# Moving the second batch's first pair forward: loads, transposes and scores in a fused attention and MoE kernel

## The chip, the cores and the metric

The kernel runs on one core of one Trainium2 chip. The metric is the device time of one execution in microseconds. Before the change the median of 7 runs is 318.27 us (317.29 to 319.65). One execution was also taken by the hardware profiler; all durations below come from it.

## What is computed

Attention with a few global tokens, followed by a two-layer feed-forward with a hard-swish gate. There are 8 batches of 8 heads, 512 local and 32 global positions, head size 64. Cut to what matters:

```python
s_g = scale * q_g @ concat(k_g, k_l).T          # global queries see all keys
out_g = softmax(s_g) @ concat(v_g, v_l)
s_ll = where(|i - j| <= 32, scale * q_l @ k_l.T, -1e9)   # local window
s_l = concat(scale * q_l @ k_g.T, s_ll)
out_l = softmax(s_l) @ concat(v_g, v_l)
x = concat(out_g, out_l) per token               # [8 * 544, 512]
h = x @ w_in                                     # 512 -> 2048
out = (h * clip(h + 3, 0, 6) / 6) @ w_out        # 2048 -> 512
```

## The kernel before, in words

Work is cut into 32 pairs p of two heads: p = 4 b + m, with b the batch and m the pair of heads in it. Pairs 0 to 3 are the first batch, pairs 4 to 7 the second. An order written out by hand covers the first two batches and is what the change edits; from pair 8 on a loop does the rest.

The steps of a pair are functions. `load` (L117) issues the DMAs of k, q and v on SP's queue into one of 16 staging buffers; `cast` (L131) turns them into 16-bit tiles kn, qn and vt; `vshift` (L142) makes a copy of v shifted by half a block, vb. `emit_T` (L216) transposes kn and qn on TensorE and copies them from PSUM: k by VectorE into kT (L229), q by ScalarE into qT (L232), with a small wrapped copy (L237 for the second batch). `emit_S(p, ch)` (L299) makes the scores of one of two chunks: two mask matmuls (L281), eight score matmuls (L293), two exps on ScalarE (L297). `emit_AV` (L324) multiplies with v and divides by the sums on VectorE (reciprocal L344, product L345, giving xn). `emit_X` (L387) transposes xn on TensorE (L398) and copies it to xt on VectorE (L402). For the global tokens `load_g`, `cast_G` (L191) and `emit_G` (L201, L209) bring keys and queries in; `kglob` (L211) copies the global keys of a batch into its kT, and `vglob` (L146) the global values into its vb. `emit_SG` (L303) makes the scores of the global queries, `emit_TD` (L241) transposes a later pair by DMA.

The feed-forward of a batch is cut into units. `u1(c)` (L421) is one of 16 columns of the first layer: four matmuls over m (L426), one activation t on ScalarE (L431), one product gt on VectorE (L433). It can be split over m: the first HEAD columns are started with m = 0, 1 and completed as the first batch's xt come in ("heads"). `u2(t, c4)` (L438) is a quarter of an output tile: four matmuls (L442). `M(n)` takes the next n units from a list. First-layer weights are 16 tiles; `load_w` and `cast_w` (L163, L174) bring them in, and columns 4 to 7 need tiles 4 to 7, and so on by fours. Output weights are 16 more tiles, cast on POOL.

Each engine runs its instructions in the order in which the code emits them. SP issues all loads in one order; POOL does nearly all casts in another; TensorE, ScalarE and VectorE follow the written order of steps. PSUM is seven buffers of one bank each for all steps: a step takes a free one and waits for the engine that empties it. Before the change ScalarE casts weight tiles 4 to 7, all eight first weight tiles are loaded ahead of pair 4, and pair 4's transposes follow u1(6).

Of the kernel before, what the change touches and what calls it, by code (L numbers as in the profile page):

```python
# [14 lines left out]
def kernel(  # L15
# [12 lines left out]
    nc = tc.nc  # L28
# [13 lines left out]
    qk_scale = 1.0 / math.sqrt(D)  # L42
# [3 lines left out]
    EXP = mybir.ActivationFunctionType.Exp  # L46
# [65 lines left out]
    st = {}  # L112
# [4 lines left out]
    def load(p, what="kqv"):  # L117
        b, m = divmod(p, NM)
        s = st.setdefault(p, {})
        for c in what:  # L120
            src = {"k": k_l, "q": q_l, "v": v_l}[c]
            t = stage()
            if c != "v" and b < NRUN:
                nc.sync.dma_start(out=t.rearrange("p (h x) -> p h x", h=2),  # L124
                                  in_=src[b, 2 * m:2 * m + 2].rearrange("h (p j) d -> p h (j d)", j=NT))
            else:
                nc.sync.dma_start(out=t.rearrange("p (h kb d) -> p (h kb) d", h=2, kb=NT),
                                  in_=src[b, 2 * m:2 * m + 2].rearrange("h (kb p) d -> p (h kb) d", p=P))
            s[c + "f"] = t.rearrange("p (h kb d) -> p kb h d", h=2, kb=NT)

    def cast(p, what, eng):  # L131
        b, m = divmod(p, NM)
        s = st[p]
        for c in what:
            if c == "v":
                o = vts[b % NV][:, :, m, vc].rearrange("p kb (h d) -> p kb h d", h=2)
            else:
                s[c + "n"] = wrk.tile([P, NT, P], FP16, tag=c + "n", name=c + "n", bufs=4)
                o = s[c + "n"].rearrange("p kb (h d) -> p kb h d", h=2)
            eng.tensor_copy(out=o, in_=s[c + "f"])  # L140
# [27 lines left out]
    def cast_w(kind, i, eng):  # L168
        if kind == "in":
            qd, m = divmod(i, NM)  # L170
            o = w_in_t[m][:, qd * 512:(qd + 1) * 512]
        else:
            o = w_out_t[i // 4][:, i % 4]
        (eng.copy if eng is nc.scalar else eng.tensor_copy)(out=o, in_=w_st[kind, i])  # L174
# [5 lines left out]
    def load_g(b0, b1, nm):  # L180
        src = {"kg": k_g, "qg": q_g}[nm]
        t = stage()
        nc.sync.dma_start(
            out=t[:, 0:(b1 - b0) * HH * D].rearrange("p (n d) -> p n d", d=D),
            in_=src[b0:b1].rearrange("b (x y) s d -> (y s) (b x) d", x=HH))
        gst[b0, nm] = t

    def cast_G(b0, b1, nm, eng=nc.vector):
        n = wrk.tile([P, 4 * P], FP16, tag="gn", name=nm + "n", bufs=2)
        nb = b1 - b0  # L190
        eng.tensor_copy(out=n[:, 0:nb * P], in_=gst[b0, nm][:, 0:nb * P])  # L191
        gst[b0, nm, "n"] = n
# [18 lines left out]
    def kglob(b, eng):  # L211
        kv = kTs[b % 2][:, :, 0:NT * KW].rearrange("p m (u c) -> p m u c", u=NT)
        eng.tensor_copy(out=kv[:, :, :, P:KW],
                        in_=kgT[:, :, b].unsqueeze(2).to_broadcast([P, NM, NT, Sg]))

    def emit_T(p, qdve=False):  # L216
        b, m = divmod(p, NM)
        s = st[p]
        kT = kTs[b % 2][:, m]
        kv = kT[:, 0:NT * KW].rearrange("p (u c) -> p u c", u=NT)  # L220
        qT = wrk.tile([P, Sl + W], FP16, tag="qT", name="qT", bufs=5)
        ps = {}
        for c in "kq":
            ps[c] = ps_tile("psT" + c, FP16)[:, 0:Sl]
            for j in range(NT):
                nc.tensor.matmul(out=ps[c][:, j * P:(j + 1) * P], lhsT=s[c + "n"][:, j], rhs=ident,
                                 is_transpose=True)
        qcopy = nc.vector.tensor_copy if qdve else nc.scalar.copy
        nc.vector.tensor_copy(  # L229
            out=kv[:, :, 0:P].rearrange("p u (i j) -> p u i j", j=NT),  # L230
            in_=ps["k"].rearrange("p (j u i) -> p u i j", j=NT, u=NT))
        qcopy(out=qT[:, W:Sl + W].rearrange("p (i j) -> p i j", j=NT),  # L232
              in_=ps["q"].rearrange("p (j i) -> p i j", j=NT))
        if b == 0:
            nc.vector.tensor_copy(out=qT[:, 0:W], in_=qT[:, Sl:Sl + W])
        else:
            nc.scalar.copy(out=qT[:, 0:W].rearrange("p (i j) -> p i j", j=NT),  # L237
                           in_=ps["q"].rearrange("p (j i) -> p i j", j=NT)[:, P - W // NT:P])
        s["qT"], s["kT"] = qT, kT
# [41 lines left out]
            nc.tensor.matmul(out=pss[e], lhsT=ident, rhs=mneg[:, ch], start=True, stop=False,  # L281
                             skip_group_check=True)

    def emit_Ss(p, ch):
        s = st[p]
        qT, kT, pss = s["qT"], s["kT"], s["ps", ch]
        if "E" not in s:
            s["E"] = wrk.tile([P, 2, 2, Sl], FP16, tag="E", name="E", bufs=3)
        for w in range(NT):
            c0 = w * KW if ch == 0 else ((w - 1) % NT) * KW + D  # L290
            for e in range(2):
                r = slice(e * D, (e + 1) * D)
                nc.tensor.matmul(out=pss[e][:, w * P:(w + 1) * P], lhsT=kT[r, c0:c0 + P],  # L293
                                 rhs=qT[r, w * P:(w + 1) * P], start=False, stop=True,
                                 skip_group_check=True)
        for e in range(2):
            nc.scalar.activation(out=s["E"][:, ch, e], in_=pss[e], func=EXP, scale=qk_scale)  # L297

    def emit_S(p, ch):  # L299
        emit_Sm(p, ch)  # L300
        emit_Ss(p, ch)
# [85 lines left out]
    def emit_X(p):  # L387
        b, m = divmod(p, NM)
        xn = st[p]["xn"]
        if b > 3 or (b == 3 and m < NM - 1):  # L390
            xt = wrk.tile([P, Sl], FP16, tag=f"xt{m}", name=f"xt{m}", bufs=2)
            xts.setdefault(b, []).append(xt)
            nc.sync.dma_start_transpose(out=xt.rearrange("p (w c) -> p w c", w=NT),
                                        in_=xn.rearrange("p w c -> p (w c)"))
            return
        psX = ps_tile("psX", FP16)
        for w in range(NT):
            nc.tensor.matmul(out=psX[:, w * P:(w + 1) * P], lhsT=xn[:, w], rhs=ident,  # L398
                             is_transpose=True)
        xt = wrk.tile([P, Sl], FP16, tag=f"xt{m}", name=f"xt{m}", bufs=2)  # L400
        xts.setdefault(b, []).append(xt)
        nc.vector.tensor_copy(out=xt, in_=psX[:, 0:Sl])  # L402
# [68 lines left out]
    def M(n):  # L471
        for _ in range(n):
            if units:
                units.pop(0)()
# [16 lines left out]
    load(3, "kq")  # L491
    for p in range(1, NM):
        load(p, "v")
    for i in range(8):
        load_w("in", i)
    load(4, "kq")
    load_g(1, 4, "kg")
    load(5, "kq")
    for i in range(8, 12):
        load_w("in", i)  # L500
    load(6, "kq")
    load(4, "v")
    load(5, "v")
    load(7, "kq")
    for i in range(12, NC):
# [41 lines left out]
    def ones_v(i, eng):  # L547
        for c in (1, 2 + P):
            eng.memset(vbs[i][0:P - W, :, :, c:c + 1], 1.0)
            eng.memset(vts[i][:, :, :, c:c + 1], 1.0)  # L550
# [16 lines left out]
    def first(p, what="kqv"):  # L567
        cast(p, what, nc.gpsimd)
        vshift(p, nc.gpsimd)
# [6 lines left out]
        first(p, "v")  # L576
    for i in range(4):
        cast_w("in", i, nc.gpsimd)
    ones_v(1, nc.gpsimd)
    vglob(1, nc.gpsimd)  # L580
    cast(4, "kq", nc.gpsimd)
    cast(5, "kq", nc.gpsimd)
    for i in range(8, 12):
        cast_w("in", i, nc.gpsimd)
    cast(6, "kq", nc.gpsimd)
    first(4, "v")
    first(5, "v")
    cast(7, "kq", nc.gpsimd)
    for i in range(12, NC):
# [13 lines left out]
    u1 = units.pop(0)  # L603
# [19 lines left out]
    emit_S(3, 0)  # L623
    emit_AV(1)
    emit_S(3, 1)
    for i in range(4, 8):
        cast_w("in", i, nc.scalar)
    emit_X(1)
    emit_AV(2)
    HEAD = 4  # L630
    for c in range(HEAD):
        u1(c, range(2))
    emit_X(2)
# [1 line left out]
    for c in range(HEAD):  # L635
        u1(c, range(2, 3))
    emit_X(3)
    for c in range(HEAD):
        u1(c, range(3, 4))
    u1(4)  # L640
    u1(5)
    u1(6)
    emit_T(4)
    cast_G(1, 4, "kg")
    emit_T(5)
    emit_G(1, 4, "kg")
    emit_S(4, 0)
    u1(7)
    kglob(1, nc.vector)
    u1(8)  # L650
    emit_S(4, 1)
    emit_T(6)
    u1(9)
    emit_S(5, 0)
    emit_AV(4)
    u1(10)
    emit_S(5, 1)
    emit_X(4)
    u1(11)
    emit_T(7)  # L660
    emit_S(6, 0)
    emit_AV(5)
    u1(12)
    emit_S(6, 1)
    emit_S(7, 0)
    emit_X(5)
    emit_AV(6)
    for t in Egs:
        nc.vector.memset(t[:, NT], 0.0)
    cast_G(0, 4, "qg")  # L670
    u1(13)
    emit_S(7, 1)
    emit_X(6)
    emit_G(0, 4, "qg")
    u1(14)
    emit_AV(7)
    u1(15)
    emit_SG(0)
    emit_SG(1)
    M(1)  # L680
    emit_TD(2 * NM)
    load(2 * NM + 1)
    cast(2 * NM + 1, "kq", nc.gpsimd)
# [1 line left out]
    emit_X(7)  # L685
    sum_E(0)
    sum_E(1)
    M(1)
    emit_SG(2)
    emit_SG(3)  # L690
    vglob(2, nc.gpsimd)
    kglob(2, nc.gpsimd)
    held = [units.pop(0), units.pop(0)]
    u2 = moe_units(lambda mm: xts[1][mm], Sl, local_dests(1))
    units[:0] = u2[0:NC]
# [144 lines left out]
```

## Time and profile before

| | |
|---|---|
| median of 7 runs | 318.27 us |
| profiled execution | 318.91 us |
| its span, first to last instruction | 317.1 us |
| TensorE busy, VectorE, ScalarE, POOL | 305.2, 212.7, 201.6, 152.0 us |
| granted TensorE clock | 1.00 |
| loads in the first 70 us | 18.25 MB at a mean of 261 GB/s |

Times in the rows are microseconds from the start of the span. A row of the timeline has the start, the time taken, the engine, the line, the operation, the tiles written and read, the shapes, and how many instructions were merged; square brackets hold the idle time of the engine before it and what ended that. A DMA row in the chain of waits runs from its issue to its landing. PE is TensorE, PEld its weight loads, DVE VectorE, ACT ScalarE, POOL GpSimd, SP the engine that issues loads.

### The profile page before, as it was taken

How to read it: one execution, taken by the hardware profiler on the slowest of the kernel's cores; microseconds unless marked ns; L12 is line 12 of the kernel's file. 1: busy time of each engine (PE TensorE's matmuls, PEld its weight loads, DVE VectorE, ACT ScalarE, POOL GpSimd, SP SyncE). 2: the span in 40 equal slices, each digit the busy share in tenths (PEclk: the TensorE clock that was granted, in tenths of full speed). 3: DMA queues.
4: the chain of work that ended last, by engine and by line, in shares of the span. 5: the costliest groups of instructions: out<-in, count | busy, mean ns of one | idle time of the engine just before them, and what ended most of it. 6: DMA issues, size and time to landing. Idle time of an engine off the chain costs nothing.

```text
span 317.1 us, 7319 instructions
## 1 busy us (share of the span) xinstructions
PE 305.2 (96%) x2673; PEld 162.0 (51%) x2673; DVE 212.7 (67%) x485; ACT 201.6 (64%) x420; POOL 152.0 (48%) x270
## 2 busy tenths in 40 slices
PE   7996999999999899999999999999999999999995
PEld 5553455545555454555555555555555554448444
DVE  6758678898665998568956896458834962389101
ACT  6757886886444895479844994589656941579000
POOL 4776788469976685575585456543410000000000
PEclk9999999999999999999999999999999999999999
DMA  7999999999999997999999997897542002100131
GB/s 211 266 283 315 253 290 276 250 173 224 179 241 204 207 226 152 189 207 189 198 174 210 209 185 155 203 198 123 112 114 86 17 19 83 66 2 1 35 99 66
DMA packets 140260, 53.05 MB, mean 167 GB/s; under 512 B 127552, under 2 KB 131904, under 8 KB 140224
## 3 DMA queue, kind: packets, MB, share of 16 engines
q1 hardware_dynamic: 138048, 52.32, 76.0%
q0 software_dynamic: 2176, 0.26, 1.3%
q8 instruction: 21, 0.34, 0.5%
q14 instruction: 15, 0.12, 0.2%
HBM read 35.13 MB, written 8.91 MB: 139 GB/s over the span
## 4 chain that ended last, share of the span: by engine, by line
PE 60%; DMA 14%; POOL 11%; DVE 5%; issue 3%; SPq 3%; ACT 2%; POOLq 0%; ACTq 0%
PE po L442 28%; PE psH L426 25%; DMA stg<-in_v_l_dram 8%; DMA stg<-in_moe_w_out_dram 4%; DVE gt L433 3%; POOL vt L140 2%; PE psS L268 2%; DMA stg<-in_k_l_dram 2%; POOL vb L144 2%; SPq L124 2%; PE pav L340 1%; PE pav L337 1%; DVE E L275 1%; POOL vb L147 1%; PE po L454 1%
## 5 line engine op out<-in xcount | busy, mean ns | idle before, releaser
L442 PE MATMUL po<-wout,gt 128*128 128x512 f16 x528 | 122.8, 379 | 0.0
L426 PE MATMUL psH<-xt,win 128*128 128x512 f16 x512 | 119.2, 379 | 2.8 <-DVE gt L433 2.1
L433 DVE SCALAR_TENSOR_TENSOR gt<-t,psH 128x512 f16<-128x512 f32 (+1 forms) x144 | 89.8, 652 | 23.0 <-ACT t L431 21.9
L431 ACT ACTIVATE t<-psH,half_col 128x512 f32<-128x512 f32 (+1 forms) x144 | 91.6, 669 | 14.7 <-PE psH L426 12.9
L426 PEld LDWEIGHTS <-win 128*128 128x128 f16 x576 | 53.1, 98 | 54.7 <-issue 2.8
L442 PEld LDWEIGHTS <-gt 128*128 128x128 f16 x528 | 48.4, 98 | 51.9
L275 DVE TENSOR_TENSOR E<-E,mk 128x512 f16<-128x512 f16 x96 | 50.3, 557 | 30.4 <-ACT E L272 28.8
L272 ACT ACTIVATE E<-psS 128x512 f16<-128x512 f32 x96 | 49.8, 604 | 13.7 <-PE psS L268 13.6
L446 ACT COPY ot<-po 128x512 f32<-128x512 f32 x16 | 9.4, 585 | 58.7 <-PE po L442 53.1
L140 POOL CAST kn<-stg 128x512 f16<-128x512 f32 x31 | 20.1, 647 | 31.8 <-DMA stg<-in_k_l_dram 31.3
L363 POOL TENSOR_TENSOR s<-Eg 128x128 f32<-128x128 f16 x24 | 10.7, 446 | 36.9 <-ACT Eg L312 35.9
L446 DVE COPY ot<-po 128x512 f32<-128x512 f32 x17 | 11.7, 690 | 23.1 <-PE po L442 23.0
L345 DVE TENSOR_TENSOR xn<-pav,rc 128x256 f16<-128x256 f32 x64 | 26.0, 421 | 1.3
L140 POOL CAST qn<-stg 128x512 f16<-128x512 f32 x31 | 19.7, 636 | 11.7 <-DMA stg<-in_q_l_dram 11.4
L140 POOL CAST vt<-stg 128x512 f16<-128x512 f32 x32 | 20.5, 641 | 8.0 <-DMA stg<-in_v_l_dram 7.3
L144 POOL COPY vb<-vt 64x512 f16<-64x512 f16 x32 | 20.0, 625 | 2.1
L297 ACT ACTIVATE E<-psS 128x512 f16<-128x512 f32 x32 | 17.1, 609 | 4.9 <-PE psS L293 4.7
L337 PE MATMUL pav<-vt,E 128*128 128x65 f16 x256 | 20.0, 194 | 0.0
L340 PE MATMUL pav<-vb,E 128*128 128x65 f16 x256 | 20.0, 195 | 0.0
L337 PEld LDWEIGHTS <-E 128*128 128x128 f16 x256 | 17.8, 99 | 3.4
L340 PEld LDWEIGHTS <-E 128*128 128x128 f16 x256 | 16.9, 97 | 2.9
L268 PEld LDWEIGHTS <-kT 64*128 64x128 f16 x384 | 10.8, 94 | 9.9 <-issue 9.2
(93 smaller groups left out, 277.3 us busy)
## 6 DMA issues: line engine op xcount, KB each, us to landing
stg<-in_k_l_dram SPq DMA_DIRECT2D x32, 256.0 KB, 3.6
stg<-in_q_l_dram SPq DMA_DIRECT2D x32, 256.0 KB, 4.2
stg<-in_v_l_dram SPq DMA_DIRECT2D x32, 256.0 KB, 4.7
out_dram<-ot SPq DMA_DIRECT2D x23, 256.0 KB, 3.9
stg<-in_moe_w_in_dram SPq DMA_DIRECT2D x16, 256.0 KB, 5.7
stg<-in_moe_w_out_dram SPq DMA_DIRECT2D x16, 256.0 KB, 4.9
out_dram<-ot SPq DMA_DIRECT2D x8, 192.0 KB, 4.0
out_dram<-ot SPq DMA_DIRECT2D x16, 64.0 KB, 1.9
```

Of the source, the lines that this page charges most:

```text
L140: eng.tensor_copy(out=o, in_=s[c + "f"])
L144: eng.tensor_copy(out=vbs[b % NV][0:D, :, m, vc], in_=vts[b % NV][D:P, :, m, vc])
L272: nc.scalar.activation(out=E[:, ch, e], in_=pss[2 * ch + e], func=EXP, scale=qk_scale)
L275: nc.vector.tensor_tensor(out=E[:, ch, e], in0=E[:, ch, e], in1=mk[:, ch].rearrange("p w c -> p (w c)"), op=mult)
L337: nc.tensor.matmul(out=o, lhsT=E[:, 0, e, w * P:(w + 1) * P], rhs=vt[:, w, m, c], start=True, stop=False, skip_group_check=True)
L340: nc.tensor.matmul(out=o, lhsT=E[:, 1, e, w * P:(w + 1) * P], rhs=vb[:, (w - 1) % NT, m, c], start=False, stop=True, skip_group_check=True)
L345: nc.vector.tensor_tensor(out=xn[:, 2 * w2:2 * w2 + 2].rearrange("p w (e d) -> p w e d", e=2), in0=po[:, :, 1:1 + P].rearrange("p w (e d) ...
L426: nc.tensor.matmul(out=ps[:, 0:n], lhsT=w_in_t[m][:, c * P:(c + 1) * P], rhs=rhs(m), start=(m == 0), stop=(m == NM - 1), skip_group_check= ...
L431: nc.scalar.activation(out=t1[:, 0:n], in_=ps[:, 0:n], func=RELU, bias=half_col, scale=1.0 / 6.0)
L433: nc.vector.scalar_tensor_tensor(out=gts[c][:, 0:n], in0=t1[:, 0:n], scalar=1.0, in1=ps[:, 0:n], op0=amin, op1=mult)
L442: nc.tensor.matmul(out=po[t][:, 0:dm], lhsT=gts[c][:, t * P:(t + 1) * P], rhs=w_out_t[c // 4][:, c % 4], start=(c == 0), stop=(c == NC - 1))
L446: (nc.scalar.copy if t % 2 else nc.vector.tensor_copy)(out=ot, in_=po[t][:, 0:dm])
```

## The change

In SP's order, pair 4's k and q and the global keys of batches 1 to 3 go ahead of weight tiles 4 to 7, and pair 4's v goes ahead of tiles 8 to 11. POOL's order follows: it casts pair 4's k and q after tile 3, then tiles 4 to 7 (before on ScalarE), pair 5's k and q, pair 4's v, and only then the constant columns and global values of the second batch's vb. On TensorE three columns are started as heads instead of four; pair 4's transposes stand between the first batch's last X and the heads' last matmuls; the global keys follow u1(3). A new step `emit_S4` makes the scores of both chunks of a pair in one run: four mask matmuls, sixteen score matmuls, four exps. The columns u1 are spread differently between the steps of pairs 4 to 7, and the first two output units move behind X(7) and SG(3).

```diff
--- before.py
+++ after.py
@@ -281,7 +281,7 @@
             nc.tensor.matmul(out=pss[e], lhsT=ident, rhs=mneg[:, ch], start=True, stop=False,
                              skip_group_check=True)
 
-    def emit_Ss(p, ch):
+    def emit_Ss(p, ch, exps=True):
         s = st[p]
         qT, kT, pss = s["qT"], s["kT"], s["ps", ch]
         if "E" not in s:
@@ -293,8 +293,21 @@
                 nc.tensor.matmul(out=pss[e][:, w * P:(w + 1) * P], lhsT=kT[r, c0:c0 + P],
                                  rhs=qT[r, w * P:(w + 1) * P], start=False, stop=True,
                                  skip_group_check=True)
+        if exps:
+            emit_Se(p, ch)
+
+    def emit_Se(p, ch):
+        s = st[p]
         for e in range(2):
-            nc.scalar.activation(out=s["E"][:, ch, e], in_=pss[e], func=EXP, scale=qk_scale)
+            nc.scalar.activation(out=s["E"][:, ch, e], in_=s["ps", ch][e], func=EXP, scale=qk_scale)
+
+    def emit_S4(p):
+        emit_Sm(p, 0)
+        emit_Sm(p, 1)
+        emit_Ss(p, 0, False)
+        emit_Ss(p, 1, False)
+        for ch in range(2):
+            emit_Se(p, ch)
 
     def emit_S(p, ch):
         emit_Sm(p, ch)
@@ -491,15 +504,17 @@
     load(3, "kq")
     for p in range(1, NM):
         load(p, "v")
-    for i in range(8):
+    for i in range(4):
         load_w("in", i)
     load(4, "kq")
     load_g(1, 4, "kg")
+    for i in range(4, 8):
+        load_w("in", i)
     load(5, "kq")
+    load(4, "v")
     for i in range(8, 12):
         load_w("in", i)
     load(6, "kq")
-    load(4, "v")
     load(5, "v")
     load(7, "kq")
     for i in range(12, NC):
@@ -576,14 +591,16 @@
         first(p, "v")
     for i in range(4):
         cast_w("in", i, nc.gpsimd)
+    cast(4, "kq", nc.gpsimd)
+    for i in range(4, 8):
+        cast_w("in", i, nc.gpsimd)
+    cast(5, "kq", nc.gpsimd)
+    first(4, "v")
     ones_v(1, nc.gpsimd)
     vglob(1, nc.gpsimd)
-    cast(4, "kq", nc.gpsimd)
-    cast(5, "kq", nc.gpsimd)
     for i in range(8, 12):
         cast_w("in", i, nc.gpsimd)
     cast(6, "kq", nc.gpsimd)
-    first(4, "v")
     first(5, "v")
     cast(7, "kq", nc.gpsimd)
     for i in range(12, NC):
@@ -623,11 +640,9 @@
     emit_S(3, 0)
     emit_AV(1)
     emit_S(3, 1)
-    for i in range(4, 8):
-        cast_w("in", i, nc.scalar)
     emit_X(1)
     emit_AV(2)
-    HEAD = 4
+    HEAD = 3
     for c in range(HEAD):
         u1(c, range(2))
     emit_X(2)
@@ -635,49 +650,44 @@
     for c in range(HEAD):
         u1(c, range(2, 3))
     emit_X(3)
+    emit_T(4)
     for c in range(HEAD):
         u1(c, range(3, 4))
+    cast_G(1, 4, "kg")
+    u1(3)
+    emit_G(1, 4, "kg")
+    kglob(1, nc.vector)
     u1(4)
+    emit_S4(4)
+    emit_T(5)
     u1(5)
+    emit_S4(5)
     u1(6)
-    emit_T(4)
-    cast_G(1, 4, "kg")
-    emit_T(5)
-    emit_G(1, 4, "kg")
-    emit_S(4, 0)
+    emit_AV(4)
+    emit_T(6)
     u1(7)
-    kglob(1, nc.vector)
+    emit_X(4)
+    emit_S4(6)
     u1(8)
-    emit_S(4, 1)
-    emit_T(6)
+    emit_AV(5)
+    emit_T(7)
     u1(9)
-    emit_S(5, 0)
-    emit_AV(4)
+    emit_X(5)
+    emit_S4(7)
     u1(10)
-    emit_S(5, 1)
-    emit_X(4)
-    u1(11)
-    emit_T(7)
-    emit_S(6, 0)
-    emit_AV(5)
-    u1(12)
-    emit_S(6, 1)
-    emit_S(7, 0)
-    emit_X(5)
     emit_AV(6)
     for t in Egs:
         nc.vector.memset(t[:, NT], 0.0)
     cast_G(0, 4, "qg")
-    u1(13)
-    emit_S(7, 1)
+    u1(11)
     emit_X(6)
     emit_G(0, 4, "qg")
-    u1(14)
+    u1(12)
     emit_AV(7)
-    u1(15)
+    u1(13)
     emit_SG(0)
     emit_SG(1)
-    M(1)
+    u1(14)
     emit_TD(2 * NM)
     load(2 * NM + 1)
     cast(2 * NM + 1, "kq", nc.gpsimd)
@@ -685,11 +695,13 @@
     emit_X(7)
     sum_E(0)
     sum_E(1)
+    u1(15)
     M(1)
     emit_SG(2)
     emit_SG(3)
     vglob(2, nc.gpsimd)
     kglob(2, nc.gpsimd)
+    M(1)
     held = [units.pop(0), units.pop(0)]
     u2 = moe_units(lambda mm: xts[1][mm], Sl, local_dests(1))
     units[:0] = u2[0:NC]
```

## The prediction

> **What bounds the kernel now.** I read the page first, then the windows of ten microseconds, the timeline of each engine up to 60 us, and last the chain that ended last. TensorE is busy for 305.2 of 317.1 us, and its idle time sits in few places:
>
> ```profile
> PE 305.2 (96%) x2673; PEld 162.0 (51%) x2673; DVE 212.7 (67%) x485; ACT 201.6 (64%) x420; POOL 152.0 (48%) x270
> ...
> 20.00:30.00 10.00, 7.11 (x61) 3.73 (x59) 7.02 (x16) 7.66 (x15) 7.07 (x13) 1.00 1.00 314
> 30.00:40.00 10.00, 9.16 (x91) 4.66 (x92) 6.80 (x16) 7.26 (x14) 6.91 (x12) 1.00 1.03 262
> 40.00:50.00 10.00, 10.00 (x136) 5.94 (x135) 7.82 (x27) 7.83 (x16) 9.12 (x16) 1.00 1.05 296
> ```
>
> The columns are the stretch, then PE, PEld, DVE, ACT, POOL busy, the granted clock, the DMA share and GB/s. TensorE lacks 2.9 + 0.8 = 3.7 us between 20 and 40 us, the place that the change works on. There the DMA engines are full and the clock is 1.00. The timelines of TensorE and ScalarE show why it idles:
>
> ```profile
> 22.91 1.32 ACT L174 CAST win<-stg 128x512 f16<-128x512 f32 x2 [0.82 <-DMA stg<-in_moe_w_in_dram]
> 24.14 4.15 ACT L431 ACTIVATE t<-psH,half_col 128x512 f32<-128x512 f32 x7
> 30.05 0.34 PE L201 MATMUL psGT<-ident,kgn 128*128 128x128 f16 x3 [1.71 <-DVE kgn L191]
> 34.21 0.40 PE L293 MATMUL psS<-qT,kT 64*128 64x128 f16 x8 [0.79 <-DVE kT L213]
> ```
>
> ScalarE casts weights until 24.1, so its seven t (L431), the seven gt of VectorE behind them and the cast kgn behind those come late, and the transposes of the global keys wait 1.71 us. From 34.2 to 106.7 us TensorE has no gap the profile lists, but one weight tile arrives with nothing to spare. In the chain of waits:
>
> ```profile
> 54.42 5.32 DMA stg<-in_moe_w_out_dram
> ...
> 59.79 0.62 POOL wout L174
> ...
> 60.46 0.38 PE po L442
> ```
>
> The last output weight lands at 59.74 and is cast by 60.4; its matmul starts at 60.46, though its unit began at 59.61 and would have reached it at 60.25. Since the DMA engines are full and the same loads precede this weight before and after, whatever TensorE gains ahead of this point ends here. The most it can win is nothing; it can lose.
>
> **The loads and POOL.** All loads go through SP's one queue in order, so a transfer that is moved takes another's place in the stream. The weight tile after the fourth lands at 20.80 (its cast on ScalarE starts at 20.83); pair 4's k takes that place, lands near 20.9 instead of 24.3, and its q near 21.6 instead of 25.1. Weight tiles 4 to 7 move to the places up to 25.7. Pair 4's v takes the place of the first of tiles 8 to 11 and lands near 28.1. POOL takes over four casts from ScalarE (0.62 us each there, 0.61 here). Its row that matters:
>
> ```profile
> 21.18 1.88 POOL L147 COPY vb<-vg 32x2048 f16<-32x2048 f16 x1
> ```
>
> Before, this copy (vglob) and the column memsets fill POOL's wait for pair 4's k. After, they stand behind pair 4's v. From 28.1 POOL has no wait left: v and its shift 1.35, memsets 0.43, vglob 1.93, four casts at 0.64 = 2.56, pair 6's k and q 1.25. The sum is 7.5, so pair 6's q is ready at 35.6, where it was at 33.1. The eighth weight tile is cast at 26.3 instead of 24.2.
>
> **TensorE up to pair 6.** Prices from rows: u1 0.86; a pair's transposes 0.46; the mask matmuls 0.95 for four at once; one chunk's scores 0.33; AV 0.50; X 0.23. Three heads end their first two parts at 19.5 and X(2), AV(3), X(3) end at 21.8. T(4) waits for its q, done at 22.6; the last head parts end at 23.2, u1(3) at 24.1. VectorE's kgn stands behind kT and three gt, and ScalarE's t behind the qT copies (0.54): gt from 24.0 at 0.6 each, kgn done near 26.2. So the 1.71 us wait stays, at about 2.1. Then come G, u1(4) to 27.2, the four scores runs of pair 4 to 28.8, T(5) 29.3, u1(5) 30.2, pair 5's scores about 31.9 (its qT stands behind four exps on ScalarE), u1(6) 32.7, AV(4) 33.2. T(6) needs POOL's q at 35.6: a wait of some 2.2 us, and T(6) ends at 35.9. Before it ended at 35.0, with more done. What is left from there to a common mark (first batch-1 work complete: all sixteen u1, X(7), SG(0) and SG(1), no output unit) is nine u1 7.8, four X 0.9, two score sets 3.2, three AV 1.5, T(7) 0.5, the global queries 0.2 and SG 0.3, together 14.4: the mark would be reached at 50.3. Before, the second output unit starts at 51.13 with one unit of 0.86 ahead of it, so its mark is 50.27. Up to here the change is worth nothing.
>
> **What the single run of scores costs.** emit_S4 queues four exps on ScalarE before the next u1's t, and gt of that u1 stands before the reciprocals of the AV that follows, in VectorE's queue. The rows:
>
> ```profile
> 9.03 2.07 ACT L297 ACTIVATE E<-psS 128x512 f16<-128x512 f32 x4
> 10.95 0.63 ACT L232 COPY qT<-psTq 128x512 f16<-128x512 f16 x1
> ...
> 36.91 0.69 DVE L433 SCALAR_TENSOR_TENSOR gt<-t,psH 128x512 f16<-128x512 f32 x1 [1.25 <-ACT t L431]
> 37.51 0.18 DVE L344 RECIPROCAL rc<-pav 128x4 f32<-128x4 f32 x1
> 37.72 0.42 DVE L345 TENSOR_TENSOR xn<-pav,rc 128x256 f16<-128x256 f32 x1
> 38.06 0.17 DVE L344 RECIPROCAL rc<-pav 128x4 f32<-128x4 f32 x1
> 38.27 0.42 DVE L345 TENSOR_TENSOR xn<-pav,rc 128x256 f16<-128x256 f32 x1
> ```
>
> Four exps hold ScalarE for 1.92 us; t takes 0.69; from the start of gt to the end of xn are 1.78 us. From the start of the first chunk's scores: 0.43 until the exps start, 1.92, 0.69, 0.04, 1.78, so xn is there after 4.86 and X is through at 5.0. Pair 6's scores are followed on TensorE by the second chunk 0.33, u1(8), AV(5), T(7), u1(9) and X(5), which would be through at 3.57: a wait of 1.4 us. Before, AV(5) follows an S of two exps with gt already done, and the profile lists no wait. Pair 7's scores are followed by u1(10), AV(6), u1(11) and X(6), through at 3.11: a wait of 1.9 us. The cast of the global queries follows xn on VectorE (memsets 0.13, cast 0.39), so their transposes wait 0.3 more, and X(7), behind gt, xt, four copies of 1.2, gt and xn, 0.15. Together 3.8 us: the mark falls at 54.0.
>
> **Sum.** 54.04 - 50.27 = 3.77 us, less the 0.2 us wait for the last weight tile, which a later TensorE no longer has: +3.6 us. TensorE has no listed gap from there to 106.7 us, so nothing takes it back; the wait of 1.52 us at 108.3 ends on gt, behind ScalarE and TensorE themselves, and moves along. The span becomes 320.7 us and the profiled run 318.91 + 3.6 = 322.5; against the median of 318.27, 321.8 us. Casts taken off ScalarE (4 x 0.62) are no gain, as they delayed only work that now waits for kgn or POOL.
>
> **Bounds.** Not shown before is which PSUM buffers the run of four takes. Best, buffers long free: nothing. Worst, pair 6's and 7's last mask waits for a buffer that gt or xt holds (free 0.9 and 1.0 us after the masks could end): +1.9. I take nothing, since three or four of seven are free by my times. DMA landings jump by up to 1.2 us in the stream (30.80 after 29.12, where 0.65 to 0.8 is usual), so POOL's 35.6 is worth 0.8 either way. Downstream, POOL's copy of 1.88 us at 104.3 lies beside VectorE's mask products (2.94 us for three, 0.51 for one before); a shifted TensorE may miss it and lose up to the 1.5 + 0.4 us of waits at 108.3 and 120.1: down to +3.6 - 0.8 - 1.9 = +0.9; up to +3.6 + 0.8 + 1.9 = +6.3 if all worst come together.
>
> The clock is 1.00 in all windows, through the gap of 1.71 us, so I charge no clock for gaps of 2.2. The Trainium skill (TensorE: Matmul & The Clock Gate, "What's actually happening") says that an idle window of about 3.4 us halves TensorE's clock until a busy one has passed. By that rule a POOL later by 1.2 us would cost an estimated 1.7 us more, and my sum would be +5.3; no gap in this trace is long enough to show it.
>
> **Rivals.** *The waits for xn do not come* (the four exps run far enough ahead, or DVE's rows are shorter): the mark is 50.3 and the last weight tile pins the rest; 318.3 us. Against it: t, gt and xn are queued in the order of the code on both engines in the trace. Chance 0.12. *Faster*: the phase shift removes the waits of 1.52 and 0.41 us at 108.3 and 120.1, since POOL's 1.88 us copy no longer stands beside the mask products. Price 1.9 us, in VectorE's stage at 103 to 108 us; it decides only if the front part loses under 1 us. 318.3 - 1.9 = 316.4 us. For it: DVE took 0.98 us per product there and 0.50 elsewhere. Against it: a loss of 3.6 ahead. Chance 0.07. *More loss* by PSUM buffers held: 318.27 + 5.5 = 323.8 us; for it, two T, four S and one u1 are seven of seven buffers. It is in the slower case. *The loads do not come earlier*: T(4) then waits to 25.8 ahead of the heads, 3.2 us more before kgn; POOL's wait for pair 6 covers about 2.2, so some 1 us is added.
>
> **How the numbers follow.** Slower by over 0.3% (0.95 us, about what a measurement of this kernel can tell from no change): 0.81, all cases with the waits for xn. Within: 0.12. Faster: 0.07. The range reaches from no change, 318.2, to 323.8, the loss with held buffers; faster at 0.07 and the far ends stay out.
>
> **What would show it.** Right: ScalarE rows of four exps (L297) at pairs 4 to 7; TensorE waits at psX (L398) on xn of 1 to 2 us, twice, near 42 and 48 us; a wait of T(6) on POOL's kn or qn near 35; kgn again a wait near 26; the last output weight landing near 59.7 with no stall on it; the later waits unchanged. Wrong: no psX waits, output weights that land earlier than 59, or a first output unit near 50.

## The result, and the profile after

The changed kernel takes 323.51 us (median of 12 runs, 321.44 to 326.51) beside 318.98 us of the kernel before (31 runs): ratio 1.0138, 95% interval 1.0114 to 1.0163, that is 3.6 to 5.2 us slower. The forecast was +3.6 us and 321.8 us. The profiled execution after has a span of 320.9 us, with 322.65 us for the run. The totals hardly move:

```profile
PE 305.8 (95%) x2673; PEld 162.7 (51%) x2673; DVE 212.7 (66%) x485; ACT 198.8 (62%) x416; POOL 153.9 (48%) x274
...
20.00:30.00 10.00, 7.92 (x82) 4.46 (x81) 7.33 (x20) 4.29 (x9) 6.46 (x12) 1.00 1.08 342
30.00:40.00 10.00, 8.17 (x91) 4.48 (x89) 4.67 (x10) 7.62 (x17) 9.74 (x19) 1.00 1.08 295
40.00:50.00 10.00, 6.73 (x81) 3.52 (x78) 5.59 (x18) 5.92 (x12) 9.58 (x18) 1.00 1.00 275
```

The first line is from the page, the others are the windows of ten microseconds. Four casts went from ScalarE to POOL. TensorE gains 0.8 us between 20 and 30 us and loses 1.0 and 3.3 us in the next two windows, where POOL is nearly full. The timeline of TensorE names the waits (in brackets: idle time before, and what ended it):

```profile
26.97 0.34 PE L201 MATMUL psGT<-ident,kgn 128*128 128x128 f16 x3 [1.80 <-DVE kgn L191]
35.62 0.40 PE L226 MATMUL psTk<-ident,kn 128*128 128x128 f16 x4 [1.46 <-POOL kn L140]
42.86 0.28 PE L411 MATMUL psX<-ident,xn 128*128 128x128 f16 x2 [1.01 <-DVE xn L358]
43.40 0.28 PE L411 MATMUL psX<-ident,xn 128*128 128x128 f16 x2 [0.26 <-DVE xn L358]
48.88 0.29 PE L411 MATMUL psX<-ident,xn 128*128 128x128 f16 x2 [1.45 <-DVE xn L358]
49.43 0.28 PE L411 MATMUL psX<-ident,xn 128*128 128x128 f16 x2 [0.26 <-DVE Eg L680]
50.18 0.40 PE L201 MATMUL psGT<-ident,qgn 128*128 128x128 f16 x4 [0.47 <-DVE qgn L191]
```

Line numbers are up to 13 higher after the change: L302 is the exps, L411 the transposes of X, L444 is t, L446 gt, L358 xn. The two pairs of psX rows are new; the wait on kgn is still there, a little longer. How xn comes late is read down the ScalarE and VectorE timelines:

```profile
38.89 2.06 ACT L302 ACTIVATE E<-psS 128x512 f16<-128x512 f32 x4 [0.73 <-PE psS L293]
40.81 0.71 ACT L444 ACTIVATE t<-psH,half_col 128x512 f32<-128x512 f32 x1
...
41.56 0.69 DVE L446 SCALAR_TENSOR_TENSOR gt<-t,psH 128x512 f16<-128x512 f32 x1 [2.34 <-ACT t L444]
42.16 0.17 DVE L357 RECIPROCAL rc<-pav 128x4 f32<-128x4 f32 x1
42.37 0.42 DVE L358 TENSOR_TENSOR xn<-pav,rc 128x256 f16<-128x256 f32 x1
```

Four exps take ScalarE from 38.89 to 40.81; t waits behind them; VectorE idles 2.34 us for t with gt at the head of its queue, and the reciprocals of AV(5), whose matmuls ended near 40.5, start at 42.16. X(5) needs xn and waits.

### The profile page after: what moved, and what is told of

Read it like the earlier page. It is cut to its first block, busy times and chain, and to the rows that moved or that the text cites. A ratio compares the mean times of both kernels' runs of the same rounds, so it can differ in the third digit from the quotient of the medians.

```text
span 320.9 us, 7313 instructions
## 1 busy us (share of the span) xinstructions
PE 305.8 (95%) x2673; PEld 162.7 (51%) x2673; DVE 212.7 (66%) x485; ACT 198.8 (62%) x416; POOL 153.9 (48%) x274
## 4 chain that ended last, share of the span: by engine, by line
PE 76%; DVE 7%; DMA 5%; ACT 4%; POOL 2%; issue 2%; SPq 1%; POOLq 0%
PE po L455 35%; PE psH L439 29%; DMA stg<-in_q_l_dram 4%; PE psS L268 3%; DVE gt L446 3%; DMA stg<-in_k_l_dram 2%; PE pav L350 2%; PE pav L353 2%; DVE xn L358 1%; ACT t L444 1%; DVE E L275 1%; PE psSG L324 1%; ACT E L302 1%; PE po L467 1%; PE pg L390 1%
## 5 line engine op out<-in xcount | busy, mean ns | idle before, releaser
L446 DVE SCALAR_TENSOR_TENSOR gt<-t,psH 128x512 f16<-128x512 f32 (+1 forms) x144 | 90.0, 650 | 27.4 <-ACT t L444 26.2
L444 ACT ACTIVATE t<-psH,half_col 128x512 f32<-128x512 f32 (+1 forms) x144 | 91.7, 670 | 19.0 <-PE psH L439 17.9
L140 POOL CAST kn<-stg 128x512 f16<-128x512 f32 x31 | 19.0, 614 | 32.3 <-DMA stg<-in_k_l_dram 29.1
L376 POOL TENSOR_TENSOR s<-Eg 128x128 f32<-128x128 f16 x24 | 10.8, 452 | 35.7 <-ACT Eg L325 34.9
L140 POOL CAST vt<-stg 128x512 f16<-128x512 f32 x32 | 21.7, 679 | 11.3 <-DMA stg<-in_v_l_dram 10.9
L358 DVE TENSOR_TENSOR xn<-pav,rc 128x256 f16<-128x256 f32 x64 | 26.0, 421 | 1.3
L144 POOL COPY vb<-vt 64x512 f16<-64x512 f16 x32 | 20.7, 648 | 2.1
L302 ACT ACTIVATE E<-psS 128x512 f16<-128x512 f32 x32 | 17.0, 603 | 5.8 <-PE psS L293 5.7
```

What stands on the lines that cost most here:

```text
L144: eng.tensor_copy(out=vbs[b % NV][0:D, :, m, vc], in_=vts[b % NV][D:P, :, m, vc])
L358: nc.vector.tensor_tensor(out=xn[:, 2 * w2:2 * w2 + 2].rearrange("p w (e d) -> p w e d", e=2), in0=po[:, :, 1:1 + P].rearrange("p w (e d) ...
L444: nc.scalar.activation(out=t1[:, 0:n], in_=ps[:, 0:n], func=RELU, bias=half_col, scale=1.0 / 6.0)
L446: nc.vector.scalar_tensor_tensor(out=gts[c][:, 0:n], in0=t1[:, 0:n], scalar=1.0, in1=ps[:, 0:n], op0=amin, op1=mult)
```

## The experiments

Theory A is the prediction's: gt, queued behind four exps on one side and ahead of AV's reciprocals on the other, makes xn and so X late. Rival B is that POOL and the loads set the pace and the wait on xn is only where it shows.

Two measures serve throughout: the ratio to the kernel before, timed on the same chip, and in the profile the mark of the prediction (all sixteen u1, X(7), SG(0) and SG(1) done). In the changed order the first output unit starts at the mark. Before it was 50.27, after it is 55.03.

**The changed kernel again.**

> The changed kernel once more, beside the other runs of this call. Both theories: ratio to the kernel before 1.011 to 1.016. Its profile tells whether the first 18 us of the profiled run after, in which TensorE was 1.0 us later than before ahead of every edit, belong to the change: if not, the scores of pair 3 start near 16.1 us again and the mark (X(7), u1(15), SG(0), SG(1) done) falls near 54.0; if so, 17.1 and 55.0 again.

Ratio 1.0133 (1.0099 to 1.0167). X(0) starts at 14.28 us, near the 14.03 of before and not at the 14.98 of the profile after, so that early delay is of single executions. The mark was at 56.69 and the span 322.6 us all the same, and the windows show a reason that neither profile of the first comparison has:

```profile
36.00:38.00 2.00, 1.84 (x13) 0.93 (x14) 1.23 (x4) 0.67 (x2) 1.87 (x4) 0.82 0.99 290
38.00:40.00 2.00, 2.00 (x9) 0.80 (x7) 1.02 (x2) 0.69 (x1) 2.00 (x5) 0.50 1.02 237
40.00:42.00 2.00, 2.00 (x27) 1.24 (x27) 0.00 (x0) 1.17 (x3) 1.94 (x5) 0.83 0.93 206
```

After a wait of 2.08 us on pair 6's k the granted clock (third number from the end) falls; 0.82, 0.50 and 0.83 make a stretch at 0.50 from 37.3 to 40.7 us. Half of 3.4 us is 1.7 us of TensorE's time. The two spans differ by as much (322.6 and 320.9), though X(0) was 0.7 us earlier here and the wait on pair 6's k 0.6 us longer.

**u1 ahead of the scores.**

```diff
-    emit_S4(6)
-    u1(8)
+    u1(8)
+    emit_S4(6)
...
-    emit_S4(7)
-    u1(10)
+    u1(10)
+    emit_S4(7)
```

> u1(8) ahead of pair 6's scores and u1(10) ahead of pair 7's, so that their t and gt no longer stand behind four exps and ahead of the reciprocals of AV(5) and AV(6). Theory A (order of the queues): the psX waits on xn (1.0 + 0.3 and 1.45 + 0.3 us) shrink to under 0.5 us together, and the kernel is 2.3 to 3.3 us faster than the changed one, ratio to before 1.003 to 1.007. Rival B (TensorE waits there for work that POOL and the loads bring late, and the xn wait is only where it shows): the wait moves to other rows, the gain stays under 1 us, ratio at or over 1.010.

Ratio 0.9996 (0.9973 to 1.0019): the whole loss is gone with two exchanges of lines, more than the 2.3 to 3.3 us expected. The timeline of TensorE has X(4), X(5) and X(6):

```profile
38.60 0.28 PE L411 MATMUL psX<-ident,xn 128*128 128x128 f16 x2 [1.00 <-DVE xn L358]
39.14 0.29 PE L411 MATMUL psX<-ident,xn 128*128 128x128 f16 x2 [0.26 <-DVE xn L358]
43.52 0.39 PE L411 MATMUL psX<-ident,xn 128*128 128x128 f16 x4
47.48 0.63 PE L411 MATMUL psX<-ident,xn 128*128 128x128 f16 x4
```

X(5) and X(6) no longer wait; X(4), where u1(6) still stands behind pair 5's four exps, now does. Rival B falls for this pair of waits. In the front a part of the loss is left: the mark is 53.66 in this profile, in which the clock fell once, against 51.92 in a profile of the kernel before with such a fall (below). That the time is level all the same was not taken apart.

**Globals early.** The memsets and the 1.88 us copy go ahead of weight tile 4 in POOL's order.

> The constant columns and the global values of the second batch (2.3 us of POOL) moved back to POOL's wait ahead of weight tile 4. Theory A: pair 6's k and q are ready 1.5 us earlier, the wait of its transposes (1.46 + 0.16 us) falls under 0.4, the xn waits stay, and the kernel is 1.0 to 1.6 us faster than the changed one, ratio to before 1.008 to 1.011. Rival B: POOL sets the whole stretch, and the xn waits shrink too: over 2 us faster. A third case: the time goes to the xn or weight waits that follow, gain under 0.5 us.

Ratio 1.0123 (1.0093 to 1.0154), no gain that can be told. Pair 6's transposes no longer wait, but X(4) does, by 1.00 and 0.26 us on xn. The POOL wait had covered the same fault at pair 5: the third case.

```profile
36.57 0.39 PE L226 MATMUL psTk<-ident,kn 128*128 128x128 f16 x4
...
39.05 0.28 PE L411 MATMUL psX<-ident,xn 128*128 128x128 f16 x2 [1.00 <-DVE xn L358]
```

**Both.**

> Both edits of the two kernels before. Theory A: the gains add, 3.5 to 4.5 us under the changed kernel, ratio to before 0.999 to 1.003, and the last output weight becomes a wait again within 0.3 us of nothing. Theory of the pin (what is won ahead of the last output weight is lost at it): the ratio does not go under 0.998 however small the other waits are. Rival B: no more than the better of the two edits alone.

Ratio 0.9994 (0.9974 to 1.0015), as the first edit alone. In both profiles the clock fell in the front, and by then pair 6's k and q were there: with the first edit alone, too, T(6) does not wait and X(4) waits 1.00 and 0.26 us, so the second edit had nothing to free at T(6). The last output weight is cast at 59.4 us and its matmul starts at 63.3, so it was no wait; the theory of the pin was not put to the test here.

**The cast of the global keys early too.** On top of both edits:

```diff
     emit_T(4)
+    cast_G(1, 4, "kg")
     for c in range(HEAD):
         u1(c, range(3, 4))
-    cast_G(1, 4, "kg")
```

> Three edits on the changed kernel: u1 ahead of the scores of pairs 6 and 7, globals early, and the cast of the global keys ahead of the three heads' gt on VectorE, so that the wait on kgn (2.4 us in the kernel with the first two edits, where the granted clock then was 0.50 for 3.4 us) shrinks to about 0.5. Theory A with the clock: no stretch at 0.50, output units begin 2 to 4 us earlier, near 50 us, and the last output weight (cast near 59.5) is a wait again; 1 to 2.5 us under the kernel before, ratio 0.992 to 0.997. Theory of the hard pin: the last output weight takes all of it, ratio 0.998 to 1.002. Rival B: the wait moves to pair 5's and 6's casts on POOL, ratio at 1.000 or over, clock drop kept.

Ratio 1.0003 (0.9976 to 1.0030): a miss in time. The wait on kgn fell to 0.58 us and the clock held, but TensorE next waits for weight tiles 4 to 7 and for pair 6's k and q (0.5 and some 0.4 us near 27 and 34 us), and the first output unit starts at 51.4. The ratio is in the range of the hard pin, but the pin is not what held it: the last output weight was cast by 59.3 us and its unit starts at 60.8.

**The gaps filled.** `warm_up(10)`, matmuls of zeros whose result is not used, ahead of the global keys' and of pair 6's transposes.

> The changed kernel with ten matmuls of zeros (128x256, 0.107 us each) ahead of the wait on kgn and ten ahead of the wait on pair 6's k: they fill 1.1 of 1.8 us and 1.1 of 1.5 to 2.1 us in which TensorE idles, and lead nowhere. If a halved clock after these gaps (0.50 from 37.3 to 40.7 us in one profile of the changed kernel, not in the other) is a part of the loss in some executions, the slowest executions vanish and the median falls by 0.4 to 1.2 us: ratio 1.009 to 1.012, clock 1.000. If the clock has no part in it, the time stays (1.013) or grows by up to 0.5 us.

Ratio 1.0143 (1.0109 to 1.0176), no gain. The profile has the clock at 1.00 after the start and a span of 320.4 us, but it is of the quickest of six executions. The other five have a mean granted clock of 0.989 to 0.995, so the clock fell in them although 1.1 us of both gaps was filled. After which wait it fell is not shown; those on xn (1.01 and 1.45 us) were still there.

**Only the loads and casts.**

> The kernel before with only the change's loads and casts: pair 4 loaded ahead of weight tiles 4 to 7, these cast on POOL, pair 4's v and the globals as in the change; TensorE's order of before. Theory A: what hurts is the run of four exps, so the loads alone cost only what pair 6's q loses (35.6 instead of 33.1, transposed at 34.5 before): about 1 us, ratio 1.000 to 1.005, and the kgn wait stays about 1.7 us although the casts have left ScalarE. Rival B (loads and POOL carry the loss): ratio 1.008 or more.

Ratio 1.0043 (1.0017 to 1.0069), some 1.4 us: the loads are the smaller part. The wait on kgn was 2.19 us although ScalarE had no casts left, and weight tiles 4 to 7, cast later on POOL, added 1.3 us in four waits. The changed order hides these waits, as it needs the tiles later, so the 1.4 us are not simply a share of the loss.

**Only the cast of the global keys early.**

> The changed kernel with only the cast of the global keys moved ahead of the heads' gt. Theory A: the kgn wait (1.8 us) goes, but pair 6's k and q still come from POOL near 35.6, so the wait there grows by as much, to 3 to 3.5 us; no time is won, ratio 1.011 to 1.016, and the longer single gap halves the clock in more executions (0.50 for 3.4 us in the profile). Rival: the kgn wait is on the path, 1.5 us won, ratio 1.008 to 1.010.

Ratio 1.0135 (1.0104 to 1.0165): no time won, as theory A said. What followed is in the timeline:

```profile
24.92 0.33 PE L201 MATMUL psGT<-ident,kgn 128*128 128x128 f16 x3
26.64 0.39 PE L439 MATMUL psH<-xt,win 128*128 128x512 f16 x1 [0.96 <-POOL win L174]
27.39 0.39 PE L439 MATMUL psH<-xt,win 128*128 128x512 f16 x1 [0.35 <-POOL win L174]
...
35.73 0.40 PE L226 MATMUL psTk<-ident,kn 128*128 128x128 f16 x4 [1.92 <-POOL kn L140]
```

The 1.8 us went to the weight tiles and to pair 6's k, which POOL had ready at 35.7 here and at 35.6 in the profile after, though TensorE came to it earlier here. The wait there was 1.92 us, not 3 to 3.5, because the tiles took their share first; the clock fell to 0.50 behind it.

**gt behind xn.** u1(8) and u1(10) stay behind the exps with matmuls and t; only their gt on VectorE goes behind AV(5) and AV(6). With `late=True`, u1 emits matmuls and t and returns gt.

```diff
-    u1(8)
+    g8 = u1(8, late=True)
     emit_AV(5)
+    g8()
...
-    u1(10)
+    g10 = u1(10, late=True)
     emit_AV(6)
+    g10()
```

> The changed kernel with u1(8) and u1(10) where they are, their t still behind four exps on ScalarE, but their gt put behind the reciprocals and products of AV(5) and AV(6) on VectorE. Theory A in its narrow form (it is VectorE's order that makes xn wait for t): the psX waits go under 0.5 us together and the kernel comes to 1.000 to 1.004 of before. Rival (ScalarE behind four exps is itself the limit, whatever VectorE's order): gain under 1 us, ratio 1.010 or more.

Ratio 1.0022 (0.9997 to 1.0047). ScalarE's order is the changed one, the run of four is there, and the loss of 1.4% shrinks to 0.2%. ScalarE and VectorE after pair 6's scores (gt is L447 here):

```profile
38.19 2.06 ACT L302 ACTIVATE E<-psS 128x512 f16<-128x512 f32 x4 [0.76 <-PE psS L293]
40.12 0.71 ACT L444 ACTIVATE t<-psH,half_col 128x512 f32<-128x512 f32 x1
...
39.63 0.18 DVE L357 RECIPROCAL rc<-pav 128x4 f32<-128x4 f32 x1 [1.15 <-PE pav L353]
...
40.86 0.69 DVE L447 SCALAR_TENSOR_TENSOR gt<-t,psH 128x512 f16<-128x512 f32 x1
```

The reciprocals start as AV's matmuls end, 39.6 instead of 42.2. So it is gt's place in VectorE's queue that makes the exps cost time. What remains is a wait of 1.07 us on the cast of the global queries, which now has a gt ahead of it.

**The kernel before again.**

> The kernel before once more, for its profile: if the wait of 1.52 us on gt near 108 us, with three mask products in 2.94 us beside POOL's copy of global values, stands again, it belongs to this kernel; if it is gone, it is of single executions. And if X(0) starts near 14.5 us, as in the profiles of all changed kernels, instead of 14.0, the early difference is none of the change's.

The time was 319.15 us. TensorE has no listed wait near 108 us (the next, 0.20 us, is at 112.4) and three mask products take 1.51 us, so the wait of 1.52 us is not in every execution of this kernel. X(0) starts at 14.27. The clock falls here too, after waits of 1.66, 0.35 and 0.42 us:

```profile
28.68 0.40 PE L226 MATMUL psTk<-ident,kn 128*128 128x128 f16 x4 [1.66 <-POOL kn L140]
...
28.00:30.00 2.00, 0.80 (x8) 0.45 (x8) 2.00 (x5) 1.07 (x4) 1.84 (x3) 0.97 1.07 349
30.00:32.00 2.00, 1.75 (x13) 0.79 (x13) 1.81 (x6) 0.54 (x2) 1.82 (x3) 0.50 1.17 240
```

Its mark is 51.92 (second output unit at 52.78, less 0.86), 1.65 us behind that of the first profile, but the span is only 0.3 us longer (317.4 and 317.1): without the wait near 108 us most of it came back. Set beside executions of the same clock, the front part loses 55.03 - 50.27 = 4.8 us and 56.69 - 51.92 = 4.8 us.

**POOL's copy later in the kernel before.** The copy of the global values at pair 12, and a second, shorter copy that follows it, behind the casts of pair 16's k and q.

> The kernel before with POOL's copy of the global values at pair 12 (1.88 us, from 104.3 us) put behind the casts of pair 16's k and q, so that it no longer lies beside the mask products of VectorE. If the products took 0.98 us each because of POOL's copy (0.38 each in the changed kernels, where the phase is another), the wait of 1.52 us at 108.3 goes: 1.0 to 1.5 us less than before, ratio 0.995 to 0.998. If they were slow for another reason, or the copy now falls on the next products, ratio 0.999 to 1.003.

Ratio 1.0026 (1.0000 to 1.0053), a miss. The wait near 108 us is absent from the kernel before run again as well, so often there may have been nothing to win. The two copies, now at 113.0 to 115.7 us, ran into the next mask products, three of which took 1.92 us. This profile has the one listed wait on the last output weight, cast at 62.15: 0.22 us.

**u1 first at three pairs.** The kernel with all three edits, and `u1(6)` ahead of `emit_S4(5)`.

> The kernel with all three edits (u1 first for pairs 6 and 7, globals early, global keys' cast early), and u1(6) ahead of pair 5's scores too. Theory A: the last waits on xn at X(4) (0.22 + 0.26 us) go, 0.3 to 0.6 us less than without it, ratio 0.997 to 1.000. Rival B: POOL's pair 6 takes it back, ratio as without it, 1.000.

Ratio 0.9937 (0.9916 to 0.9957), 317.12 beside 319.21 us: faster than both kernels, by 1.4 to 2.7 us against before. The waits on xn at X(4) to X(6) are gone from the profile, as are those on pair 6's k and q:

```profile
30.00:40.00 10.00, 10.00 (x118) 5.95 (x117) 6.45 (x16) 8.88 (x20) 8.61 (x16) 1.00 1.12 289
...
58.42 1.03 PE L455 MATMUL po<-wout,gt 128*128 128x512 f16 x4
```

TensorE is busy for the whole of 30 to 40 us, the first output unit starts at 49.08, and the unit with the last output weight runs without a wait at 58.4, since that weight was cast by 57.4 us here. In none of the six runs did the clock fall (1.000 in all). The gain is larger than the 0.3 to 0.6 us expected for this last edit; no run takes it apart further.

## Why the prediction was right

**The main step held.** The prediction put the loss into gt standing between four exps and the reciprocals of AV. From the start of pair 6's scores (38.46) X(5) was through at 43.52, 5.06 us against 5.0; for pair 7 from 44.48 to about 49.55, 5.07. The waits at X(5) and X(6) were 1.27 and 1.71 us against 1.4 and 1.9. Exchanging u1 with the scores, or moving gt alone, takes 1.1 to 1.4 of the 1.4% back. The rival that xn would not wait falls.

**The front held in kind.** kgn was a wait again (1.80 us against 2.1), pair 6's transposes were held by POOL, and taking the kgn wait alone away won nothing. T(6) ended at 36.4 instead of 35.9: pair 4's v landed near 29.1, not 28.1, so POOL's row of work without a wait started later. With the cast of the global queries (0.67 us instead of 0.39, and a wait of 0.47 instead of 0.3) the mark came at 55.03 instead of 54.0.

**Terms that were mis-sized.** The sum for the front was 3.8 us and it measured 4.8. The 1.52 us wait near 108 us, which was to move along, was absent from the profile after: between the scores at 101.8 and at 118.7 (106.4 and 122.5 after), 0.8 us of the lead came back. With the 0.2 us of the last output weight, 4.8 - 0.8 - 0.2 is the +3.8 us that this pair of spans shows, against a forecast of 3.6.

**The term that was left out.** The clock was charged nothing "through the gap of 1.71 us": the gap did not halve the clock in the one profile that was there, but gaps of 1.66 to 2.4 us did in others. The mean granted clock of every timed run tells how often: 0.998 or more without a fall, 0.992 to 0.995 with one, 0.989 or less with two. It fell in 38 of 69 runs of the kernel before and in 12 of 18 of the changed kernel, but not at the same price. One fall goes with 0.1 us in the kernel before (means of 319.3 and 319.4 us) and with 1.4 us in the changed one (322.4 and 323.8; 325.6 with two). Without a fall the change costs some 3 us, with runs from several chips set side by side; so of the 4.4 us measured about one came with the clock. That the total came within 0.8 us of the forecast is in part luck: the front and the clock cost more than the sum held, and 0.8 us came back near 108 us. The cause does not hang on the clock: without a fall, u1 ahead of the scores and gt behind xn are at 319.3 and 319.1 us.

**A step that failed without deciding.** "The most it can win is nothing" took the landing of the last output weight as fixed by the order of the loads. Its cast ended at 59.6 to 62.2 us in the four profiles with TensorE's order of before and at 57.4 to 59.4 in the ten with a changed one, and the best kernel reached the unit at 58.4 with no wait. In the profile after it was cast by 58.8, so a sign that the prediction had named for being wrong, output weights that land before 59, came together with the signs for being right. The weight is a near bound, not a hard one; a change in front of it can win. The chance for slower did not rest on this, as the loss came from elsewhere. A slip in the bounds did not matter either: by its own figures, 29.12 and 30.80, the jump of landings is 1.7 us, not 1.2.

## What to carry to other kernels

Batching work on one engine is priced by what stands behind it on the next one: follow the first instruction after the batch into the other engine's queue, and see what is queued behind its consumer. Here two exchanges of lines, or the place of two products, were worth 1.1 to 1.4%, while TensorE, ScalarE and VectorE did the same work. And before a late input is called the bound, look at what would wait next: a POOL wait of 1.5 us that was removed came back as a wait of 1.3 us of the kind it had hidden.

## What the runs showed of the hardware

**The clock after short gaps.** In 8 of 14 profiles of these kernels, before and changed ones, the granted clock was 0.50 for 3.4 us once after the front waits, and in one of them again at 114 us. In all six profiles with a single wait of 1.9 us or more ahead (1.92 to 2.36 us) it fell; after 1.66 to 1.80 us it fell in two and held in three; with no front wait over 0.9 us it held. The length of one wait does not decide alone. The two profiles of the kernel before have waits of 0.40, 0.31 and 1.71 us, after which it held, and of 1.66, 0.35 and 0.42 us, after which it fell; and by the mean clock it held in 8 of 12 runs of the kernel with both edits, whose profile has 2.36 us. The Trainium skill (TensorE: Matmul & The Clock Gate, "What's actually happening") gives about 3.4 us of idle time before the clock halves. The length of the slow stretch agrees with its figure for the busy window, the idle time does not: no gap here was over 2.4 us, so the measurement decides.

**Mask products beside a POOL copy.** Three products took 2.94 us in the profile before, beside POOL's copy at 104.3 us, and 1.11 to 1.92 us in the other 13 profiles, where this copy was over or still to come. The 1.11 us are of the profile with POOL idle beside them; shorter casts and copies lay beside the 1.92 us:

```profile
104.60 2.94 DVE L275 TENSOR_TENSOR E<-E,mk 128x512 f16<-128x512 f16 x3
...
106.27 1.51 DVE L275 TENSOR_TENSOR E<-E,mk 128x512 f16<-128x512 f16 x3
```

The first is from the profile before, the second from the same kernel run again, with one cast beside it. One profile alone shows the long copy beside them. Whether they meet changes from one execution to the next, with the time at which loads land.
